# Two heads' matrix products interleaved by kind: maxima, scores and biases of an attention kernel in mixed pairs

## The chip, the core and the metric

The kernel runs on one core of one Trainium2 chip. The metric is the device time of one execution in microseconds (us), from one launch that computes everything. TensorE (PE in the profile) multiplies matrices, with its weight loads shown as PEld; VectorE (DVE), ScalarE (ACT) and GpSimd (POOL) work on elements; SyncE (SP) here only starts the stores of the output.

## What is computed

Attention over 8 batches and 12 heads with 448 tokens of 64 features each, and then a soft mixture of 8 experts with 4 slots each:

```python
scores = scale * np.matmul(q, k.transpose(0, 1, 3, 2))
m = np.max(scores, axis=-1, keepdims=True)
e = np.exp(scores - m)
attn = e / (np.sum(e, axis=-1, keepdims=True) + np.exp(-m) + 1e-09)
attn_out = np.matmul(attn, v)
x = attn_out.transpose(0, 2, 1, 3).reshape(B * S, H * D)
logits = x @ phi                       # 3584 x 32
slot_input = softmax(logits, axis=0).T @ x
slot_out = relu(slot_input @ w1) @ w2  # one pair of matrices for each of 8 experts
out = softmax(logits, axis=1) @ slot_out
```

Inputs and output are float32; the kernel multiplies in bfloat16.

## The kernel before

The 96 heads are handled as 48 pairs (NPAIR). The 64 features of one head of a pair lie in partitions 0 to 63 and those of the other in 64 to 127, so that a product of either head uses half of TensorE's rows, and two such products, one in each half, can run side by side. `hl` is the head in the pair, 0 or 1.

For a pair, four kinds of work go through TensorE:

- `T(n)` transposes q and k of pair n (28 small products, line 205) into one bank of PSUM. ACT (line 208) copies it out for one pair in three, DVE (line 210) for the other two.
- `A(n, i)` makes the row maxima: for one chunk i of 128 queries the products with all 448 keys (line 227, one for each head), each into a bank of its own, and for each a reduction on DVE (line 231) into one column of `mx`. The last chunk, i = 3, has 64 queries for each head and puts both heads into one bank (lines 237 and 240). A pair's four `A` are called runs of maxima here.
- `Bk(n, i)` makes the transposed scores of one chunk i of 128 keys with all queries (line 302, one product for each head), adds the negated maxima to them by a second product with a selecting matrix into the same bank (line 305, called the bias), and takes the exponential on ACT (line 308), one instruction for each head. The chunk i = 3 has 64 keys for each head.
- `AV(n, i, ...)` multiplies the exponentials with v (line 339); `N1` copies the result out (line 351, on ACT for all but the last pairs), `N2` normalises it (lines 360 and 361 on DVE, then lines 367 to 376 on POOL), and `PX` transposes it for the second part of the kernel (line 399, copied out by ACT at line 405).

PSUM's banks come from three pools, each handed out in turn: `psA` with three banks (transposes, maxima products, and the small products of the second part), `psB` with four (scores, `PX`, and the transposed maxima), `psV` with one (`AV`). A product that takes a bank waits until the instruction that empties the bank's former content is through. TensorE takes its products in the order in which they stand in the program, which is written out by hand.

The main loop runs over s = 0 to 48, a step for each pair, with two halves, y = 0 (the early half) and y = 1 (the late half). The scores are those of pair s, the maxima run some pairs ahead: from s = 3 on exactly four pairs, so that at step s the maxima are those of pair s + 4. The list `runs` holds the runs of maxima still to do, and `As(c)` does the next c of them. From s = 3 on a step does this on TensorE:

```python
# y = 0
As(1); Bk(s, 0); Bk(s, 1); As(1)           # maxima 0, scores 0 and 1, maxima 1
AV(s - 1, 2 and 3)                         # with post[2 * s] among it, where there is one
# y = 1
As(1); Bk(s, 2); Bk(s, 3, side=1)          # maxima 2, scores 2, scores 3 with maxima 3 within
T(s + 6); W2 and W3 in every third step; AV(s, 0 and 1); post[2 * s + 1]; PX(s - 2)
```

`W1` (line 247, on POOL) negates the maxima of three pairs, `W2` (lines 267 and 268) transposes them, `W3` (lines 273 to 279) copies them out. `post` holds the parts of the second half of the kernel, spread over the steps of the next batch of six pairs: the logits (line 434, copied by ACT at line 438), their maxima (lines 442, 452, 463, 465), exponentials (lines 474 and 479) and the sums over the tokens (line 489, added by DVE at line 499). After step 47 the experts' matrices, whose last parts are loaded by then, are multiplied and the output is made and stored.

Loads are issued from POOL's queue: q, k and v some steps ahead, and the experts' matrices (line 108) in parts over the whole loop.

Of the kernel before, what the change touches and what calls it, by code (L numbers as in the profile page):

```python
# [8 lines left out]
F32 = mybir.dt.float32  # L9
BF16 = mybir.dt.bfloat16  # L10
AX = mybir.AxisListType
AF = mybir.ActivationFunctionType
# [12 lines left out]
HG = 6  # L25
# [6 lines left out]
def kernel(  # L32
# [10 lines left out]
    nc = tc.nc  # L43
    B, H, S, D = q.shape
# [9 lines left out]
    NPAIR = B * PB  # L54
    NG = NPAIR // NP
    scale = 1.0 / (D ** 0.5)
# [15 lines left out]
    sel = const.tile([128, HG], BF16, name="sel")  # L72
# [6 lines left out]
    NQK, NE, VPN, NATV = 7, 5, HG * 4 * VS, HG * 4 * D  # L79
# [11 lines left out]
    e2_t = [part("e2", i * 2 * S, 2 * S).rearrange("p (h s) -> p h s", h=2) for i in range(NE)]  # L91
# [30 lines left out]
    with ExitStack() as at:  # L122
# [3 lines left out]
        psA = pool("psA", 3, space=PSUM)  # L126
        psB = pool("psB", 4, space=PSUM)
        psV = pool("psV", 1, space=PSUM)
        pb_ = lambda nm: psB.tile([128, 512], F32, tag="b", name=nm)
# [55 lines left out]
        mx, ngm, ec, mT, eT, av, us = {}, {}, {}, {}, {}, {}, {}  # L185
        qkT = {}
        st = {"e2": 0}
# [7 lines left out]
        def T(n):  # L195
            g, pl = divmod(n, NP)
            ps = psA.tile([128, 2, S], BF16, tag="a", name="ps_t")
            for a in range(2):
                src = nat["qk"[a], g]
                for tok in range(7):  # L200
                    for hl in range(2):

                        c = kcol(hl, tok) if a else (2 * tok if tok < 4 else 2 * tok - 7) * 64
                        r = slice(64 * hl, 64 * hl + 64)
                        nc.tensor.transpose(ps[r, a, c:c + 64], src[r, pl, tok * D:(tok + 1) * D], ident[r, r])  # L205
            t = qk_t[n % NQK]
            if n < 6 or pl == 0:
                nc.scalar.copy(t, ps)  # L208
            else:
                nc.vector.tensor_copy(t, ps)  # L210
            qkT[n] = t
# [3 lines left out]
        mg = lambda n: 0 if n == 0 else n // NP + 1  # L215
        mpl = lambda m: ((0, 1), (1, NP))[m] if m < 2 else (0, NP)

        def A(n, i):
            g, pl = mg(n), n % NP
            if pl == mpl(g)[0] and i == 0:  # L220
                mx[g] = psm.tile([128, 21], F32, tag="mx", name="mx")
            t = qkT[n]
            if i < 3:
                pss = [psA.tile([128, 512], F32, tag="a", name="ps_a") for _ in range(2)]
                for hl in range(2):
                    r = slice(64 * hl, 64 * hl + 64)
                    nc.tensor.matmul(pss[hl][:, 0:S], t[r, 0, i * 128:(i + 1) * 128], t[r, 1, :],  # L227
                                     start=True, stop=True)
                for hl in range(2):
                    c = HG * i + 2 * pl + hl  # L230
                    nc.vector.reduce_max(mx[g][:, c:c + 1], pss[hl][:, 0:S], axis=AX.X)  # L231
            else:
                ps = psA.tile([128, 512], F32, tag="a", name="ps_a")

                for hl in range(2):
                    r = slice(64 * hl, 64 * hl + 64)
                    nc.tensor.matmul(ps[64 - 64 * hl:128 - 64 * hl, 0:S], t[r, 0, 384:448], t[r, 1, :],  # L237
                                     start=True, stop=True)
                c = 3 * HG + pl
                nc.vector.reduce_max(mx[g][:, c:c + 1], ps[:, 0:S], axis=AX.X)  # L240
# [39 lines left out]
            ec[g] = e  # L280


        def Bk(n, i, c=0):

            g, pl = divmod(n, NP)
            t = qkT[n]
            rs = [slice(0, 64), slice(64, 128)]
            if i < 3:
                pss = [pb_("ps_b") for _ in range(2)]
                outs = [p[:, 0:S] for p in pss]  # L290
                cols = slice(i * 128, (i + 1) * 128)
                e = e2_t[st["e2"] % NE]
                st["e2"] += 1
                es = [e[:, hl, :] for hl in range(2)]
            else:
                pss = [pb_("ps_b")]
                outs = [pss[0][r, 0:S] for r in rs]
                cols = slice(384, 448)
                es = [e1_t]
            m = cols.stop - cols.start  # L300
            for hl in range(2):
                nc.tensor.matmul(outs[hl], t[rs[hl], 1, cols], t[rs[hl], 0, :], start=True, stop=False)  # L302
            As(c)
            for hl in range(2):
                nc.tensor.matmul(outs[hl], sel[rs[hl], 2 * pl + hl:2 * pl + hl + 1].to_broadcast([64, m]), mT[mg(n)][rs[hl], :],  # L305
                                 start=False, stop=True)
            for p, e in zip(pss, es):
                nc.scalar.activation(e, p[:, 0:S], AF.Exp, scale=scale)  # L308
            for hl in range(2):
                eT[n, i, hl] = es[hl % len(es)]  # L310
# [236 lines left out]
        runs = [(n, i) for n in range(NPAIR) for i in range(4)]  # L547

        def As(c):
            for _ in range(min(c, len(runs))):  # L550
                A(*runs.pop(0))
# [23 lines left out]
        for s in range(NPAIR + 1):  # L575
            for y in range(2):
                hs = 2 * s + y
                early = int(hs < 5)
                As(1)
                if s < NPAIR:  # L580
                    Bk(s, 2 * y)
                    As(early)
                    side = int(y == 1 and len(runs) > 0 and runs[0][1] == 3)
                    Bk(s, 2 * y + 1, side)
                    As(1 - side)
                else:
                    As(1)
                if hs == 1:
                    W1(1)
                if hs < 5:  # L590
                    T(hs + 3)
                if y == 0:
                    if 0 <= s - 1:
                        for i in (2, 3):
                            AV(s - 1, i, range(3))
                else:
                    if 2 <= s < NPAIR - 6:
                        T(s + 6)
                    g = (s + 1) // 3
                    if (s + 1) % 3 == 0 and g < NG:  # L600
                        W2(g + 1)
                        W3(g + 1)
                    if s < NPAIR:
                        for i in (0, 1):
                            AV(s, i, range(3))
                if 2 * s + y in post:
                    post[2 * s + y]()
                if y and 0 <= s - 2 < NPAIR - 2:
                    PX(s - 2)
                if y == 0:  # L610
                    if 0 <= s - 1:
                        for i in range(4):
                            AV(s - 1, i, [3])
                        N1(s - 1)
                        if not on_pool(s - 1):
                            N2(s - 1)
                else:
                    if 0 <= s - 1 and on_pool(s - 1):
                        N2(s - 1)
                As(early)  # L620
                if hs == 1:
                    W2(1)
                    W3(1)
                if hs == 4:
                    W1(2)
            g = (s + 10) // 3
            if s == 1 or (s and s % 3 == 2):
                if g < NG:
                    load(g, "q")
                    load(g, "k")  # L630
            g = (s + 9) // 3
            if s % 3 == 0 and g - 2 < NG:
                V(g - 2)
                if s and g - 1 < NG:
                    load(g - 1, "v")
            if s % 3 == 1:
                if 1 < (s + 2) // 3 < NG:
                    W1((s + 2) // 3 + 1)
                if s == 1:
                    load(2, "v")  # L640
            if s in half_at:
                load_half(half_at[s], 0, w_tile(half_at[s]))
            if s - 1 in half_at:
                load_half(half_at[s - 1], 1)
            for i, z0, z1 in part_at.get(s, ()):
                load_part(i, z0, z1)
# [57 lines left out]
        pss = [pb_("ps_so") for _ in range(2)]  # L704
# [5 lines left out]
        for half in range(2):  # L710
            for bp in range(B // 2):
                o = (half * (B // 2) + bp) * 4
                nc.tensor.matmul(ps_cs[:, o:o + 4], cT[:, bp, half, :, :].rearrange("p b j -> p (b j)"), band,
                                 start=True, stop=True)
# [7 lines left out]
        for half in range(2):  # L722
            hs = slice(half * ND, (half + 1) * ND)
            ps = psA.tile([128, 512], F32, tag="a", name="ps_sel")
# [5 lines left out]
    with ExitStack() as ex:  # L730
        psO = ex.enter_context(tc.tile_pool(name="psO", bufs=4, space=PSUM))
        for bp in range(B // 2):
# [4 lines left out]
            for t0 in range(0, 7, 2):  # L737
                ts = range(t0, min(t0 + 2, 7))
                pss = [psO.tile([128, 2, 512], F32, tag="o", name="ps_o") for _ in ts]
                for hf in range(2):  # L740
                    for t, ps in zip(ts, pss):
                        r = slice(32 * (t % 4), 32 * (t % 4) + NS)
                        nc.tensor.matmul(ps[:, hf, 0:ND], cT[r, bp, t // 4, :, :].rearrange("p b j -> p (b j)"),  # L743
                                         slot_out[r, hf * ND:(hf + 1) * ND], start=True, stop=True)
                for t, ps in zip(ts, pss):
                    dst = o[:, t, :].rearrange("p (h d) -> p h d", h=2)
                    c = cscale[:, t // 4, bp, t % 4:t % 4 + 1]
# [37 lines left out]
```

## Time and profile before

| | |
|---|---|
| time, median of 3 runs | 321.62 us (321.37 to 322.61) |
| time of the profiled execution | 321.49 us |
| its span, first to last instruction | 319.7 us |
| busy: PE, DVE, ACT, POOL | 284.4, 253.0, 250.1, 194.6 us |
| mean granted clock of TensorE | 0.951; 1.00 in every window up to 250 us |
| the maxima's reductions, line 231 | 288 of 615 ns, 160.7 us busy |
| the exponentials, line 308 | 336 of 560 ns, 158.3 us busy |
| maxima products, line 227 | 288, 364 ns each |
| scores and biases of full chunks, lines 302 and 305 | 288 each, 353 and 352 ns |

A row of the profile names the line of the kernel, the engine, the operation, the tile written and the tile read, and the shape; for a product "64*128 64x448" means 64 rows and 128 columns of the array and 448 columns streamed through. Timelines merge instructions of one line that follow each other closely; the count stands behind an x. The end of a product is modelled, and a product's duration is longer than the distance to the next one, since products follow each other while the former is still on its way. In square brackets stands idle time of the whole engine before the row, and what ended it. The window of a stage gives busy times that merge overlapping instructions.

### The profile page before, as it was taken

The numbers are of one execution on the slowest core, as the hardware profiler recorded it, in microseconds if no ns is written. First come the engines' busy times: TensorE is split into PE (matmuls) and PEld (weight loads), VectorE is DVE, ScalarE is ACT, GpSimd is POOL, SyncE is SP. The second block draws the span as 40 slices with busy tenths as digits, with TensorE's granted clock in tenths as the row PEclk, the third lists the DMA queues.
The fourth block names the chain that finished last, engine by engine and source line by source line (L and its number), as shares of the span: only waits on it lengthen the run. The fifth ranks groups of instructions, "written<-read, shape, count | busy, mean of one in ns | idle before, by whom it ended". The sixth has DMA issues, their size and how long they took to land.

```text
span 319.7 us, 12146 instructions
## 1 busy us (share of the span) xinstructions
PE 284.4 (89%) x5072; PEld 165.9 (52%) x5074; DVE 253.0 (79%) x575; ACT 250.1 (78%) x546; POOL 194.6 (61%) x402
## 2 busy tenths in 40 slices
PE   2898999999999999999999999999999997997800
PEld 1444556555566566656656665566555555561100
DVE  5888999998989989997999799989998354337910
ACT  2367699999989998999999999999998983217800
POOL 8651797868768968695978688867775723100000
PEclk9999999999999999999999999999999999897555
DMA  7990799999999999678999999997445899964998
GB/s 87 143 135 4 105 208 203 187 193 162 184 180 162 197 148 180 86 112 146 187 154 187 180 170 162 182 193 130 76 51 100 149 157 193 200 126 178 425 431 344
DMA packets 32838, 54.30 MB, mean 170 GB/s; under 512 B 2576, under 2 KB 27920, under 8 KB 32272
## 3 DMA queue, kind: packets, MB, share of 16 engines
q0 software_dynamic: 31776, 42.52, 81.8%
q1 hardware_dynamic: 1008, 11.01, 8.2%
q8 instruction: 39, 0.64, 0.7%
q14 instruction: 15, 0.12, 0.1%
HBM read 85.03 MB, written 11.01 MB: 300 GB/s over the span
## 4 chain that ended last, share of the span: by engine, by line
PE 53%; DVE 22%; ACT 11%; issue 4%; DMA 3%; POOL 2%; POOLq 0%; ACTq 0%
DVE mx L231 15%; PE ps_b L302 11%; PE ps_av L339 11%; PE ps_a L227 9%; PE ps_b L305 7%; PE ps_t L205 5%; ACT R L308 5%; DMA R<-in_moe_w_dram 3%; PE ps_s L489 3%; PE ps_o L743 3%; ACT R L208 2%; DVE mx L240 2%; DVE R L210 2%; ACT R L405 2%; ACT W L749 2%
## 5 line engine op out<-in xcount | busy, mean ns | idle before, releaser
L308 ACT ACTIVATE R<-ps_b 128x448 bf16<-128x448 f32 x336 | 158.3, 560 | 13.4 <-PE ps_b L305 9.9
L231 DVE TENSOR_REDUCE mx<-ps_a 128x1 f32<-128x448 f32 x288 | 160.7, 615 | 9.5 <-PE ps_a L227 9.0
L302 PE MATMUL ps_b<-R 64*128 64x448 bf16 (+1 forms) x384 | 82.6, 358 | 2.1 <-ACT R L405 1.8
L305 PE MATMUL ps_b<-mT,sel 64*128 64x448 bf16 (+1 forms) x384 | 78.9, 352 | 0.0
L227 PE MATMUL ps_a<-R 64*128 64x448 bf16 x288 | 68.8, 364 | 5.3 <-DVE mx L231 2.9
L367 POOL TENSOR_TENSOR R<-ubuf,rec 128x384 bf16<-128x384 f32 x44 | 36.3, 824 | 47.9 <-DVE rec L361 22.4
L339 PE MATMUL ps_av<-R 128*128 128x65 bf16 (+1 forms) x1536 | 64.8, 196 | 0.1
L339 PEld LDWEIGHTS <-R 128*128 128x128 bf16 (+1 forms) x1536 | 50.2, 100 | 23.9 <-issue 19.7
L205 PEld LDWEIGHTS <-R 64*64 64x64 bf16 x1344 | 31.1, 113 | 16.6 <-issue 6.1
L205 PE MATMUL ps_t<-ident,R 64*64 64x64 bf16 x1344 | 31.5, 197 | 5.3 <-DMA R<-in_q_dram 4.3
L302 PEld LDWEIGHTS <-R 64*128 64x128 bf16 (+1 forms) x384 | 19.4, 97 | 30.5 <-issue 25.6
L305 PEld LDWEIGHTS <-sel 64*128 64x128 bf16 (+1 forms) x384 | 21.3, 97 | 23.2 <-issue 15.9
L405 ACT CAST R<-ps_x 128x512 bf16<-128x512 f32 x47 | 27.9, 593 | 6.3 <-PE ps_x L399 6.2
L240 DVE TENSOR_REDUCE mx<-ps_a 128x1 f32<-128x448 f32 x48 | 29.6, 617 | 0.4 <-PE ps_a L237 0.3
L208 ACT COPY R<-ps_t 128x896 bf16<-128x896 bf16 x20 | 18.4, 918 | 10.8 <-PE ps_t L205 10.8
L351 ACT COPY ubuf<-ps_av 128x455 f32<-128x455 f32 x44 | 25.1, 571 | 1.2 <-PE ps_av L339 1.0
L227 PEld LDWEIGHTS <-R 64*128 64x128 bf16 x288 | 17.8, 94 | 14.5 <-issue 3.6
L376 POOL TENSOR_TENSOR R<-ubuf,rec 128x128 bf16<-128x128 f32 x44 | 17.6, 400 | 3.7
L237 PE MATMUL ps_a<-R 64*64 64x448 bf16 x96 | 18.5, 381 | 0.6 <-DVE mx L231 0.6
L399 PE MATMUL ps_x<-ident,R 128*128 128x128 bf16 x192 | 18.7, 218 | 0.0
L247 POOL TENSOR_SCALAR R<-mx 64x6 bf16<-64x6 f32 (+5 forms) x51 | 13.6, 266 | 8.1 <-DVE mx L231 4.7
L108 POOL DMA_DIRECT2D R<-in_moe_w_dram x15 | 8.4, 566 | 15.7 <-PE ps_s L489 6.7
(126 smaller groups left out, 368.5 us busy)
## 6 DMA issues: line engine op xcount, KB each, us to landing
W<-in_moe_w_dram POOLq DMA_DIRECT2D x22, 768.0 KB, 10.2
out_dram<-W SPq DMA_DIRECT2D x3, 2688.0 KB, 11.2
R<-in_v_dram POOLq DMA_DIRECT2D x32, 192.0 KB, 6.0
R<-in_q_dram POOLq DMA_DIRECT2D x15, 336.0 KB, 6.0
R<-in_k_dram POOLq DMA_DIRECT2D x15, 336.0 KB, 7.3
R<-in_moe_w_dram POOLq DMA_DIRECT2D x3, 768.0 KB, 7.7
out_dram<-W SPq DMA_DIRECT2D x3, 768.0 KB, 4.3
R<-in_moe_w_dram POOLq DMA_DIRECT2D x1, 1344.0 KB, 11.5
```

The costliest lines, as they stand in the source:

```text
L205: nc.tensor.transpose(ps[r, a, c:c + 64], src[r, pl, tok * D:(tok + 1) * D], ident[r, r])
L208: nc.scalar.copy(t, ps)
L227: nc.tensor.matmul(pss[hl][:, 0:S], t[r, 0, i * 128:(i + 1) * 128], t[r, 1, :], start=True, stop=True)
L231: nc.vector.reduce_max(mx[g][:, c:c + 1], pss[hl][:, 0:S], axis=AX.X)
L240: nc.vector.reduce_max(mx[g][:, c:c + 1], ps[:, 0:S], axis=AX.X)
L302: nc.tensor.matmul(outs[hl], t[rs[hl], 1, cols], t[rs[hl], 0, :], start=True, stop=False)
L305: nc.tensor.matmul(outs[hl], sel[rs[hl], 2 * pl + hl:2 * pl + hl + 1].to_broadcast([64, m]), mT[mg(n)][rs[hl], :], start=False, stop=True)
L308: nc.scalar.activation(e, p[:, 0:S], AF.Exp, scale=scale)
L339: nc.tensor.matmul(o, eT[n, i, hl][:, qc], vp[g % 2][:, 2 * pl + hl, i, 0:W65], start=(i == 0 and u == 0 and hl == 0), stop=(i == 3), skip ...
L351: (nc.scalar.copy if on_pool(n) else nc.vector.tensor_copy)(u, src)
L367: eng.tensor_mul(x[:, 0:3, c:c + 128].rearrange("p i (h d) -> p i h d", h=2), u[:, 0:6, 0:D].rearrange("p (i h) d -> p i h d", h=2), rec[: ...
L405: nc.scalar.copy(xT[:, pb, :], pss[0])
```

## The change

`A` gets a form that returns its two products, each with its reduction, as two steps, and `Bk` a form that places them among its own four products. For a full chunk (i < 3) of the scores with a full run of maxima, TensorE's order becomes

- before: maxima 0, maxima 1; score 0, score 1; bias 0, bias 1
- after: maxima 0, score 1; score 0, bias 1; bias 0, maxima 1

where the figure is the head, which is the half of the rows. Each exponential is issued behind its own bias, head 1 first. In the early half the second run of maxima used to stand behind both chunks of scores; now its first product stands ahead of the second chunk's scores and its second behind that chunk's last bias. In the late half the 64-wide chunk with its run of maxima stays as it was. The new order holds for s = 3 to 43, 41 steps with three such chunks each, which is 123 chunks; before s = 3 and after s = 43 the order is the old one. The orders of DVE, POOL and SP stay, and on ACT the two heads of a chunk's exponentials change places.

```diff
--- before.py
+++ after.py
@@ -215,11 +215,22 @@
         mg = lambda n: 0 if n == 0 else n // NP + 1
         mpl = lambda m: ((0, 1), (1, NP))[m] if m < 2 else (0, NP)
 
-        def A(n, i):
+        def A(n, i, steps=False):
             g, pl = mg(n), n % NP
             if pl == mpl(g)[0] and i == 0:
                 mx[g] = psm.tile([128, 21], F32, tag="mx", name="mx")
             t = qkT[n]
+            if steps:
+                m = mx[g]
+
+                def run(hl):
+                    r = slice(64 * hl, 64 * hl + 64)
+                    ps = psA.tile([128, 512], F32, tag="a", name="ps_a")
+                    nc.tensor.matmul(ps[:, 0:S], t[r, 0, i * 128:(i + 1) * 128], t[r, 1, :], start=True, stop=True)
+                    c = HG * i + 2 * pl + hl
+                    nc.vector.reduce_max(m[:, c:c + 1], ps[:, 0:S], axis=AX.X)
+
+                return [lambda: run(0), lambda: run(1)]
             if i < 3:
                 pss = [psA.tile([128, 512], F32, tag="a", name="ps_a") for _ in range(2)]
                 for hl in range(2):
@@ -280,11 +291,36 @@
             ec[g] = e
 
 
-        def Bk(n, i, c=0):
+        def Bk(n, i, c=0, mix=False):
 
             g, pl = divmod(n, NP)
             t = qkT[n]
             rs = [slice(0, 64), slice(64, 128)]
+            if i < 3 and mix and runs and runs[0][1] < 3:
+
+                e = e2_t[st["e2"] % NE]
+                st["e2"] += 1
+                cols = slice(i * 128, (i + 1) * 128)
+                a0, a1 = A(*runs.pop(0), steps=True)
+                pss = {}
+
+                def score(hl):
+                    pss[hl] = pb_("ps_b")
+                    nc.tensor.matmul(pss[hl][:, 0:S], t[rs[hl], 1, cols], t[rs[hl], 0, :], start=True, stop=False)
+
+                def bias(hl):
+                    nc.tensor.matmul(pss[hl][:, 0:S], sel[rs[hl], 2 * pl + hl:2 * pl + hl + 1].to_broadcast([64, 128]),
+                                     mT[mg(n)][rs[hl], :], start=False, stop=True)
+                    nc.scalar.activation(e[:, hl, :], pss[hl][:, 0:S], AF.Exp, scale=scale)
+                    eT[n, i, hl] = e[:, hl, :]
+
+                a0()
+                score(1)
+                score(0)
+                bias(1)
+                bias(0)
+                a1()
+                return
             if i < 3:
                 pss = [pb_("ps_b") for _ in range(2)]
                 outs = [p[:, 0:S] for p in pss]
@@ -576,8 +612,15 @@
             for y in range(2):
                 hs = 2 * s + y
                 early = int(hs < 5)
-                As(1)
-                if s < NPAIR:
+                mix = s >= 3 and len(runs) > 1 and runs[0][1] == 2 * y
+                if mix:
+                    Bk(s, 2 * y, mix=True)
+                    Bk(s, 2 * y + 1, y, mix=True)
+                else:
+                    As(1)
+                if mix:
+                    pass
+                elif s < NPAIR:
                     Bk(s, 2 * y)
                     As(early)
                     side = int(y == 1 and len(runs) > 0 and runs[0][1] == 3)
```

## The prediction

> **What bounds the kernel now.** I read the windows of the page's stage that the change touches first, then its waits, then the timeline of TensorE alone, last the other engines around one stall. The stage is steps s = 3 to 43, 41 steps of about 5.1 us. Its window (columns: length, then busy time of PE, PEld, DVE, ACT, POOL, the granted clock, the DMA share, GB/s):
>
> ```profile
> 39.30:246.70 207.40, 203.29 (x3937) 126.38 (x3934) 190.21 (x431) 194.37 (x441) 159.21 (x320) 1.00 0.97 159
> ```
>
> TensorE looks full, ACT is idle for 13.0 us and DVE for 17.2 us. The waits of the same window make TensorE's own waits look like nothing:
>
> ```profile
> PE ps_b L302 <- ACT R L405: 1.8, 8, 0.3
> PE ps_a L227 <- DVE mx L231: 1.1, 6, 0.2
> ```
>
> They hide it: one product uses half of the array's rows, and while the product of one half waits, the last one of the other half still counts as busy. The timeline of TensorE shows it (start, length, shape, count):
>
> ```profile
> 163.11 0.85 PE L227 MATMUL ps_a<-R 64*128 64x448 bf16 x2
> 163.61 0.53 PE L302 MATMUL ps_b<-R 64*128 64x448 bf16 x2
> ...
> 164.26 0.38 PE L302 MATMUL ps_b<-R 64*64 64x448 bf16 x2
> 164.27 0.38 PE L237 MATMUL ps_a<-R 64*64 64x448 bf16 x2
> ...
> 164.66 0.60 PE L205 MATMUL ps_t<-ident,R 64*64 64x64 bf16 x28
> ...
> 165.89 0.36 PE L227 MATMUL ps_a<-R 64*128 64x448 bf16 x2
> 166.09 0.35 PE L302 MATMUL ps_b<-R 64*128 64x448 bf16 x2
> ...
> 166.47 0.35 PE L302 MATMUL ps_b<-R 64*128 64x448 bf16 x1
> 167.01 0.35 PE L302 MATMUL ps_b<-R 64*128 64x448 bf16 x1 [0.19 <-ACT R L405]
> 167.02 0.53 PE L305 MATMUL ps_b<-mT,sel 64*128 64x448 bf16 x2
> 167.22 0.52 PE L227 MATMUL ps_a<-R 64*128 64x448 bf16 x2
> 167.67 0.79 PE L339 MATMUL ps_av<-R 128*128 128x65 bf16 x20
> 168.39 0.36 PE L227 MATMUL ps_a<-R 64*128 64x448 bf16 x2
> 168.59 0.35 PE L302 MATMUL ps_b<-R 64*128 64x448 bf16 x2
> 168.78 0.35 PE L305 MATMUL ps_b<-mT,sel 64*128 64x448 bf16 x2
> 169.06 0.38 PE L302 MATMUL ps_b<-R 64*64 64x448 bf16 x2
> ```
>
> From 168.39 on is the undisturbed case: a pair takes one pass, 0.20 us for the first, 0.19 for each further, 0.28 for the last before products of another shape. So the early half of a step (six passes) should last 1.24 us and the late half's three 0.67. At 163.11 the second maxima product started 0.50 late, though the row calls it one group of 0.85, and it held back scores that waited for nothing: 1.15 instead of 0.67. At 165.89 the half took 1.78: one score of the second pair waited 0.54 for its bank, and three passes stood behind it. Summed so over all 41 steps, early halves lose 11.0 us and late ones 6.3: 17.3 us in which half of the array stands still.
>
> The rows of the three other engines that the sum below uses, of the unfiltered timeline there and ten us later:
>
> ```profile
> 163.90 1.15 DVE L231 TENSOR_REDUCE mx<-ps_a 128x1 f32<-128x448 f32 x2
> 165.55 0.92 ACT L208 COPY R<-ps_t 128x896 bf16<-128x896 bf16 x1
> 166.33 0.63 ACT L405 CAST R<-ps_x 128x512 bf16<-128x512 f32 x1
> 173.41 0.96 POOL L247 TENSOR_SCALAR R<-mx 128x36 bf16<-128x36 f32 x3
> ```
>
> **What the change moves.** No instruction is added or dropped, DVE's and POOL's orders stay, and ACT only swaps the heads of an exponential pair. On TensorE 123 chunks (41 steps by 3) go from pairs of like products to a0+s1, s0+b1, b0+a1 (a maxima, s score, b bias, the figure is the head). Cost of the pairs themselves: nothing, six products are three passes either way, and the pairs occur already where a stall had skewed two halves. The row at 163.61 shows a score started 6 ns after the late maxima product, at 167.02 a bias product runs beside a score, at 167.22 a maxima beside a bias, and the next pass still comes 0.19 to 0.20 later. Two things differ: a waiting second maxima product no longer has its chunk's scores and biases behind it, and ACT's first exponential needs the second pass, not the third, so it may start 0.19 earlier. Against that, a maxima product now stands ahead of the second chunk's scores.
>
> **The sum,** followed from 163 to 182, the free part of a six-step cycle of 30.7 us. Releases read off the rows: a product is usable 0.39 after its start, a reduction frees its bank 0.66 after its start, reductions follow each other at 0.53.
> - Late half, 163.11. The second maxima product still starts at 163.61, since DVE sets that, but the rest is through: the 64-column step starts at 163.89, not 164.26. The transposes need the bank of the reduction of 163.90: 164.57 instead of 164.66, so TensorE keeps only 0.09. ACT keeps more: its bias is ready at 163.31 + 0.39 = 163.70, ACT is free of the copy before at 163.96, against 164.26: 0.30.
> - So L208 starts at 165.24 and L405 at 166.02, and the waiting score at 166.70 rather than 167.01. Behind it now stand two passes instead of three: last pass 166.89, next kind 167.17 instead of 167.67. Gain 0.50.
> - Next step: nothing waits in its late half; transposes 0.48 earlier; the last maxima product of the early half at 170.72 waits for DVE as before. Gain still 0.48.
> - Its late half at 172.93: DVE lets the second maxima product go at 172.98 instead of 173.46; the 64-column step comes 0.28 after that, at 173.26 instead of 174.11. Gain 0.85.
> - There POOL limits: L247 ends at 174.37, and the product that needs its last part was at 175.23 and comes to 174.38 to 174.41. Its slack is used up; 0.82 stays.
> - Early half at 175.94, now 175.12: the last maxima product waits for the first reduction, 175.12 + 0.40 + 0.66 = 176.18, next kind 176.46 instead of 177.39. Gain 0.93. DVE, idle for 1.40 us at 180.2 until TensorE's L489 is through, takes this over.
>
> From 181 to 193 the reductions are back to back (one idle of 0.28 us), and TensorE's waits there are DVE's in both orders: I take nothing. Where a stall goes is hence clear: to the last maxima product of the early half, which waits for the reduction of the first.
>
> Moving a maxima product ahead of a score costs nothing as long as its bank, freed by the copy of the last transposes, is free 0.58 after the half's start: slack 0.17 us where ACT copies (L208 from 165.24 to 166.21 with its release, due 166.38), about 0.24 where DVE does.
>
> Taking 0.9 us per six steps, 41 steps give 6.2 us. The profiled execution was 321.49 us, its span 319.7, so 1.8 lie around it; the median is 321.62, the same within 0.1%. Forecast 321.5 - 6.2 = 315.3. The start and the end of the kernel keep their length and shift.
>
> **Rivals.**
> - *Evacuation sets the pace.* DVE is at 92% and ACT at 94% of the stage, and the gain of 0.30 or 0.84 goes into waits for reductions. Against it: both engines have idle rows that TensorE ended (1.40 us above). If only the two 0.09 us ends survive, 0.2 per six steps, the gain is 1.4 and the time 320.1. [...] The trace half agrees: from 181 to 193 it is so, from 163 to 181 not.
> - *Slower: a maxima product blocks the second chunk's scores.* Its bank waits for the copy of the transposes. In the order of before, L208 ended at 166.47, exactly when the new order wants it. If L208 starts later than 0.39 us before the half, scores and thus ACT wait. One ACT instruction too late, 0.42 us, in every third step: 14 times 0.42 is 5.9 us, 327.4. For it: DVE and ACT have little room. Against it: the sum above starts L208 0.56 us before the half.
> - *Slower by much: pairs of unlike products don't run side by side.* Each of 123 x 3 passes would take 0.19 more: 70 us, 391. The rows at 163.61, 167.02 and 167.22 speak against it; so it is left with little. That the change does nothing is excluded, since TensorE's order does change in 123 places.
> - *All goes well.* The gain is bounded by ACT's idle 13.0 us: 308.5.
>
> **How the numbers follow.** Forecast 0.64; evacuation 0.20, half of it below the 0.5% (1.6 us) that a measurement can tell from no change; blocked scores 0.08; serial pairs 0.04; all gained 0.04. Faster by over 0.5%: 0.64 + 0.04 + 0.11 = 0.79; within: 0.09; slower: 0.12. The range takes the forecast with its size uncertain from under half (a gain of 2.5) to 10.5, and the evacuation case's 320.1, and leaves out the two slower cases and the best one: 311.0 to 321.0.
>
> **What would show it.** Right: L227's second product no longer holds L302 back; late halves last 0.67 or end 0.28 after the last maxima product; the early halves' first exponential starts about 0.59 after the half's first product instead of 0.77; ACT's busy share of the stage rises from 94% to 96%; waits of "PE ps_a L227" for DVE move to the end of the early half. Wrong: a first maxima product of a chunk waiting for L208 or L210 with scores behind it; a pass longer than 0.20 us; DVE's idle time in the stage not falling from 17.2 us by about 6.

## The result, and the profile after

The changed kernel takes 317.16 us (median of 19 runs, 315.17 to 320.55), the kernel before 321.9 us in the same session (19 runs, 320.79 to 323.26): the ratio is 0.9842 [0.982, 0.9863], a gain of about 5 us or 1.6%. The ratio leaves out the two slowest of the 19 runs, the profiled one among them. The forecast was 315.3 us in a range of 311.0 to 321.0. The profiled execution of the changed kernel took 320.22 us, span 318.4; it lost nearly 5 us at the very end, to a load that came late. Its stage of 41 steps is within 1.0 us of the others', so the stage is read here and the end apart.

The window of the stage, after (length, then busy time of PE, PEld, DVE, ACT, POOL, the granted clock, the DMA share, GB/s):

```profile
40.20:242.00 201.80, 200.96 (x3951) 125.18 (x3948) 188.98 (x433) 192.35 (x443) 159.00 (x321) 1.00 0.99 164
```

The stage lost about 6 us. ACT's idle time went from 13.0 to 9.45 us (201.80 - 192.35), DVE's from 17.2 to 12.8. Two waits that DVE and ACT had for TensorE in the stage of before, from the view of waits of that window,

```profile
DVE mx L231 <- PE ps_a L227: 5.9, 22, 0.6
ACT R L308 <- PE ps_b L305: 3.6, 12, 0.3
```

are nearly gone in the same view after:

```profile
DVE mx L231 <- PE ps_a L229: 1.8, 7, 0.3
ACT R L314 <- PE ps_a L229: 0.2, 1, 0.2
```

The timeline of TensorE after, at about the place of the prediction's rows (L229 maxima, L309 scores, L312 biases, L338, L341 and L248 the 64-column scores, biases and maxima, L205 the next pair's transposes, L375 `AV`):

```profile
160.51 0.35 PE L229 MATMUL ps_a<-R 64*128 64x448 bf16 x1
160.51 0.53 PE L309 MATMUL ps_b<-R 64*128 64x448 bf16 x2
160.71 0.52 PE L312 MATMUL ps_b<-mT,sel 64*128 64x448 bf16 x2
161.04 0.35 PE L229 MATMUL ps_a<-R 64*128 64x448 bf16 x1
161.31 0.38 PE L338 MATMUL ps_b<-R 64*64 64x448 bf16 x2
...
161.53 0.35 PE L341 MATMUL ps_b<-mT,sel 64*64 64x448 bf16 x2
162.00 0.63 PE L205 MATMUL ps_t<-ident,R 64*64 64x64 bf16 x28
...
163.25 0.36 PE L229 MATMUL ps_a<-R 64*128 64x448 bf16 x1
163.25 0.55 PE L309 MATMUL ps_b<-R 64*128 64x448 bf16 x2
163.45 0.54 PE L312 MATMUL ps_b<-mT,sel 64*128 64x448 bf16 x2
163.64 0.54 PE L229 MATMUL ps_a<-R 64*128 64x448 bf16 x2
...
164.32 0.35 PE L229 MATMUL ps_a<-R 64*128 64x448 bf16 x1
164.60 0.79 PE L375 MATMUL ps_av<-R 128*128 128x65 bf16 x20
```

The late half at 160.51 is the stalled kind: its second maxima product comes 0.53 later, where it was 0.50 in the kernel before, but scores and biases have gone through meanwhile, and the 64-column step follows 0.27 after it, 0.80 from the half's start. The early half at 163.25 lasts 1.35: its last maxima product, at 1.07, closes it alone.

Adding up every half beyond its undisturbed length (1.24 and 0.67 us), and the time from one kind of product to the next for all of TensorE, gives the whole account of the stage, first maxima product of s = 3 to last full one of s = 43:

| us | before | after |
|---|---|---|
| stalls in 41 early halves | 10.98 | 6.92 |
| stalls in 41 late halves | 6.32 | 1.65 |
| last 64-column bias to the transposes, summed | 7.31 | 9.63 |
| stage | 205.56 | 199.36 |
| a cycle of six steps, in the steady part | 30.67 | 29.83 |

The halves gave 8.7 us; 2.3 came back as a wait of the transposes for their bank, which a reduction empties (the row at 162.00 comes 0.47 after the last bias, where 0.19 is the undisturbed distance); every other sum, such as that of the `AV` products, is the same within 0.4 us. What is left, 6.4, is nearly the 6.2 us of the stage. In the five other profiled executions with the new order (experiments 2 and 7 to 10) the stage took 199.7 to 200.4, a gain of 5.1 to 5.9. Experiment 9 shows where such a difference can lie: in one step TensorE stands idle for 0.88 us, from 210.47, for no cause that the profile shows.

Then the end. The chain of waits of before and of after, and the timeline of TensorE after, all around the last load of the experts' matrices and the 41 products that need it:

```profile
275.17 11.12 DMA R<-in_moe_w_dram
...
286.34 1.96 PE ps_so L687 x41
```
```profile
269.12 14.46 DMA R<-in_moe_w_dram
283.62 3.44 PE ps_so L730 x36
```
```profile
278.79 1.30 PE L730 MATMUL ps_so<-R,W 128*32 128x384 bf16 x24
283.62 3.42 PE L730 MATMUL ps_so<-R,W 128*32 128x384 bf16 x41 [3.53 <-DMA R<-in_moe_w_dram]
```

The load was issued 6.05 us earlier than before, and the last of the products that need nothing of it began 6.06 earlier (278.79 against 284.85). But the load took 14.46 us instead of 11.12; TensorE stood idle for 3.53 us, and then the 41 products took 3.42 instead of 1.95 us, with the granted clock at 0.50 up to 286.6, where it was 1.00 before the change. So 6.06 - 3.4 - 1.5, about 1.2 us, was left of the gain in that execution: 321.49 - 320.22.

That 6.06 is so near to the 6.2 of the stage is chance, as the span taken apart shows (with experiments 7 and 9, the changed kernel again):

| us | before | after | 7 | 9 |
|---|---|---|---|---|
| start, up to the first maxima product of s = 3 | 39.35 | 40.58 | 40.50 | 39.48 |
| stage | 205.56 | 199.36 | 200.06 | 200.36 |
| from there to the experts' first product (L673, L716) | 30.56 | 29.47 | 30.55 | 30.25 |
| experts' products, up to L725 or L768 | 12.76 | 17.57 | 12.88 | 13.26 |
| the rest | 31.47 | 31.47 | 31.46 | 31.47 |

The start took 39.2 to 39.5 us in seven of the thirteen profiles and 40.5 to 40.8 in six, with executions of both orders in each group. In the six, the 28 transposes at 22.2 us still take 0.96 us as those before them do; in the seven, those at 21.4 to 21.7 take 0.63. The third row has two lengths too, of which the three profiles with the order of before have only the longer; the last section shows the clock there.

### The profile page after: what moved, and what is told of

Its sections match the earlier page's. It is cut to its first block, busy times and chain, and to the rows that moved or that the text cites. A ratio compares the mean times of both kernels' runs of the same rounds, so it can differ in the third digit from the quotient of the medians.

```text
span 318.4 us, 12144 instructions
## 1 busy us (share of the span) xinstructions
PE 282.9 (89%) x5072; PEld 165.1 (52%) x5074; DVE 251.1 (79%) x575; ACT 247.3 (78%) x546; POOL 194.0 (61%) x402
## 4 chain that ended last, share of the span: by engine, by line
PE 67%; DVE 14%; ACT 5%; DMA 5%; issue 3%; POOL 2%; POOLq 0%; ACTq 0%
PE ps_av L375 15%; PE ps_a L229 10%; PE ps_t L205 7%; PE ps_b L309 6%; PE ps_b L312 6%; DVE mx L231 6%; PE ps_b L338 5%; DMA R<-in_moe_w_dram 5%; PE ps_b L341 3%; DVE mx L242 3%; PE ps_x L435 3%; PE ps_s L525 3%; PE ps_o L786 2%; ACT W L792 2%; PE ps_a L238 2%
## 5 line engine op out<-in xcount | busy, mean ns | idle before, releaser
L314 ACT ACTIVATE R<-ps_b 128x448 bf16<-128x448 f32 x246 | 118.5, 576 | 0.2 <-PE ps_a L229 0.2
L229 PE MATMUL ps_a<-R 64*128 64x448 bf16 x246 | 79.9, 351 | 0.0
L309 PE MATMUL ps_b<-R 64*128 64x448 bf16 x246 | 67.8, 352 | 0.3
L312 PE MATMUL ps_b<-mT,sel 64*128 64x448 bf16 x246 | 65.5, 350 | 0.0
L375 PE MATMUL ps_av<-R 128*128 128x65 bf16 (+1 forms) x1536 | 65.1, 196 | 0.1
L375 PEld LDWEIGHTS <-R 128*128 128x128 bf16 (+1 forms) x1536 | 50.4, 101 | 27.5 <-issue 23.2
L344 ACT ACTIVATE R<-ps_b 128x448 bf16<-128x448 f32 x90 | 47.6, 573 | 7.1 <-PE ps_b L341 7.0
L205 PEld LDWEIGHTS <-R 64*64 64x64 bf16 x1344 | 31.2, 113 | 18.8 <-issue 7.5
L205 PE MATMUL ps_t<-ident,R 64*64 64x64 bf16 x1344 | 32.0, 198 | 5.6 <-DMA R<-in_q_dram 4.1
L441 ACT CAST R<-ps_x 128x512 bf16<-128x512 f32 x47 | 28.2, 600 | 7.9 <-PE ps_x L435 7.9
L251 DVE TENSOR_REDUCE mx<-ps_a 128x1 f32<-128x448 f32 x48 | 29.5, 615 | 0.6 <-PE ps_a L248 0.3
L338 PE MATMUL ps_b<-R 64*64 64x448 bf16 (+1 forms) x138 | 28.9, 380 | 0.1
L229 PEld LDWEIGHTS <-R 64*128 64x128 bf16 x246 | 23.1, 94 | 9.8
L208 ACT COPY R<-ps_t 128x896 bf16<-128x896 bf16 x20 | 18.8, 941 | 11.3 <-PE ps_t L205 11.0
L341 PE MATMUL ps_b<-mT,sel 64*64 64x448 bf16 (+1 forms) x138 | 27.0, 362 | 0.0
L312 PEld LDWEIGHTS <-sel 64*128 64x128 bf16 x246 | 20.0, 94 | 12.4 <-issue 2.2
L338 PEld LDWEIGHTS <-R 64*64 64x64 bf16 (+1 forms) x138 | 7.3, 101 | 23.2 <-issue 22.1
```

What stands on the lines that cost most here:

```text
L229: nc.tensor.matmul(ps[:, 0:S], t[r, 0, i * 128:(i + 1) * 128], t[r, 1, :], start=True, stop=True)
L309: nc.tensor.matmul(pss[hl][:, 0:S], t[rs[hl], 1, cols], t[rs[hl], 0, :], start=True, stop=False)
L312: nc.tensor.matmul(pss[hl][:, 0:S], sel[rs[hl], 2 * pl + hl:2 * pl + hl + 1].to_broadcast([64, 128]), mT[mg(n)][rs[hl], :], start=False, s ...
L314: nc.scalar.activation(e[:, hl, :], pss[hl][:, 0:S], AF.Exp, scale=scale)
L375: nc.tensor.matmul(o, eT[n, i, hl][:, qc], vp[g % 2][:, 2 * pl + hl, i, 0:W65], start=(i == 0 and u == 0 and hl == 0), stop=(i == 3), skip ...
```

## The experiments

Several theories stood. T: the order works through its waits, as in the prediction's walk. L: part of the gain, or the missing part of it, is the last load. S: each stall is worth its length. V: the stage itself varies from run to run. M: only the mixing of kinds counts. P: it only counts that the maxima stand behind. The variants called light leave out the load of seven of the eight parts of the last expert's second matrix, so that the end doesn't blur them, and don't compute the whole output; e1 and e2 are the two kernels in that form.

**1 and 2. Both kernels without the last load.**

```diff
-        load_part(15, 1, 5)
-        load_part(15, 5, 8)
```

> The kernel before, without its last two loads of the last expert's second matrix (seven of that matrix's eight row groups are left out, 1344 KB). Theory T (the attention stage gave 6.06 us, and what the end gives back is a race between TensorE and the last load): before, TensorE waited 0.19 us for that load, so 321.4. Rival L (the loads bound the end in both kernels): over 2 us below the kernel before.

> The changed kernel, with the same two loads left out. T: the whole gain of the attention stage arrives, 6.1 us below the light kernel before, 315.3, in every run within about 0.5 us. Rival V (the attention stage itself varies from run to run): the runs spread from 315 to 320 as those of the changed kernel do.

Before without it: 321.8 us (10 runs, 319.98 to 323.36), ratio 0.9975 [0.995, 1.0]. After without it: 316.3 (4 runs, 315.43 to 317.04), ratio 0.9809 [0.9776, 0.9841]. The load costs the kernel before next to nothing, so the gain isn't the load's. The changed kernel's median is 0.9 lower without it, but the intervals of the two ratios overlap, and the forecast is 1.0 lower still. That the runs lie closer together without the load isn't shown: the four here lie within 1.6 us, the four of experiment 7, with the load, within 0.6. V holds in part: the stage took 199.4 to 200.4 us in the six profiles of the changed order.

**3 and 4. The new order in one half of each step only**, both light.

```diff
-                mix = s >= 3 and len(runs) > 1 and runs[0][1] == 2 * y
+                mix = y == 1 and s >= 3 and len(runs) > 1 and runs[0][1] == 2 * y
```

and `y == 0` in the other.

> The light kernel with the new order in the late halves alone (y = 1). Walking the six-step cycle as in the prediction: ACT's 0.30 us earlier at 163 arrives at the waiting score of the next early half (0.31), and the late half at 172.93 adds 0.37: 0.68 us per six steps, 4.6 us in all, 316.8. Rival S (each stall is worth its length, so that the early halves, which lose 11.0 us, count more than the late ones with 6.3): under 3 us of gain, over 318.4.

> The light kernel with the new order in the early halves alone (y = 0). By the same walk: 0.19 us behind the score that waits for L405, 0.09 at the last maxima product of the early half at 175.94: 0.3 us per six steps, 2.0 us in all, 319.4. Rival S: over 3 us of gain, under 318.4.

The late half alone: 318.86 us (7 runs), 0.9889 [0.9854, 0.9924]; the early half alone: 320.61 (10 runs), 0.9955 [0.9933, 0.9978]. By the first maxima product of each step in the profiles:

| us | before, light | late only | early only | both |
|---|---|---|---|---|
| first 8 steps | 39.3 | 39.1 | 38.2 | 37.9 |
| a steady cycle of six steps | 30.67 | 29.97 | 30.47 | 29.8 |
| stage | 205.32 | 202.20 | 203.30 | 200.19 |
| stalls, early and late halves | 10.96, 6.30 | 9.48, 1.43 | 8.47, 6.92 | 6.86, 1.63 |

The steady cycle gains 0.70 from the late half (the walk says 0.68) and 0.20 from the early (0.3). Each half's stalls shrink where its order is changed, those of the late half to a quarter. Both times missed all the same: 318.86 for 316.8 and 320.61 for 319.4. What I missed with experiment 3 is the multiplication: its cycle doesn't hold for all 41 steps, as the first eight steps gain only 0.2 from the late half, and 1.1 from the early one; and step 38 alone was 0.5 us longer than in the light kernel before. By its time experiment 3 is on S's side (over 318.4), but S said that the early halves count more, and they gave less. The two stages add up, in one profiled execution each: 3.1 + 2.0 us, and both together gain 5.1.

**5. The second maxima product in the middle** of the three pairs, the kinds still mixed (light).

```diff
                 a0()
                 score(1)
                 score(0)
+                a1()
-                bias(1)
                 bias(0)
-                a1()
+                bias(1)
```

> The light kernel with another order of unlike pairs: a0+s1, s0+a1, b0+b1, so that the second maxima product again stands ahead of its chunk's biases. Theory T (it is the place of the second maxima product that counts, and ACT's start with the second pass): half of the gain is lost, about 3 us remain, 318.3. Rival M (it is the mixing of kinds in a pass that counts): all of it stays, 315.3.

321.45 us (10 runs, 318.98 to 323.41), 0.9976 [0.9947, 1.0006]: the gain is gone. M is out. T said 318.3, and missed by the other half of the gain. The timeline of TensorE in this kernel, an early half:

```profile
165.89 0.35 PE L229 MATMUL ps_a<-R 64*128 64x448 bf16 x1
165.90 0.79 PE L309 MATMUL ps_b<-R 64*128 64x448 bf16 x2
166.39 0.35 PE L229 MATMUL ps_a<-R 64*128 64x448 bf16 x1
166.53 0.39 PE L312 MATMUL ps_b<-mT,sel 64*128 64x448 bf16 x2
166.85 0.79 PE L375 MATMUL ps_av<-R 128*128 128x65 bf16 x20
```

The chunk's second maxima product waits till 166.39, 1.08 after the half's start at 165.31, and the two biases follow only at 166.53: the half lasts 1.54, against 1.35 in the new order. Summed, early halves stall for 14.6 us, more than before the change (11.0); late ones are down to 1.75. The steady cycle is 30.61.

**6. Like pairs, maxima last** (light): no mixing at all, but the waiting products stand at the end.

```diff
+                score(0)
+                score(1)
+                bias(0)
+                bias(1)
                 a0()
-                score(1)
-                score(0)
-                bias(1)
-                bias(0)
                 a1()
```

> The light kernel with pairs of like kinds and the maxima behind: s0+s1, b0+b1, a0+a1. No maxima product holds back a score or a bias of its chunk, and ACT starts with the second pass. Theory T: slower than before, since the first maxima product, and with it DVE, comes 0.39 us later in every half: the last maxima product of the early half waits until 1.45 us instead of 1.07, and the transposes for the reduction of the late half's first product: 0.3 to 0.6 us a step over 41 steps, 332 to 345. Rival P (all that matters is that maxima products stand behind scores and biases): as fast as the changed kernel, 315.3.

340.13 us (4 runs), 1.0573 [1.0535, 1.0611], within T's range; P is out. The timeline of TensorE there:

```profile
165.31 0.35 PE L341 MATMUL ps_b<-mT,sel 64*64 64x448 bf16 x2
165.88 0.63 PE L205 MATMUL ps_t<-ident,R 64*64 64x64 bf16 x28 [0.22 <-DVE mx L231]
...
168.66 0.35 PE L229 MATMUL ps_a<-R 64*128 64x448 bf16 x1 [0.22 <-DVE mx L231]
```

DVE gets its first banks two passes later (the first maxima product at 167.52 in the half that starts at 167.13, 0.39 us), so both the last maxima product of the half and the transposes wait for it. Of the four orders measured, only that of the change lets one maxima product go at once and the other last; like pairs with the maxima in the middle were not tried.

**7 to 11. The end.** The changed kernel twice more (7 and 9), and both kernels with the last part of the final products' order changed: first all that doesn't need the last load, for both halves of the output, then what does (8 and 10 on the changed kernel, 11 on the one before).

```diff
-            slots(1, range(FK), [half])
+            slots(1, range(5), [half])
+        for half in range(2):
+            slots(1, range(5, FK), [half])
```

> The changed kernel itself, to compare the next one with on one chip. T: 315.3 to 320, depending on how long the last load takes.

> The changed kernel with the products of the second expert group (L730) in another order: row groups 0 to 4 for both halves of the columns first, then 5 to 7 for both, so that 40 products instead of 20 stand ahead of the wait for the last load. T (the last load and TensorE race at the end): where the load is late, the 20 products (about 0.95 us) move into the wait: 0.5 to 1 us below the changed kernel in the median. Rival: no difference, as the load ends in time in most runs, or slower by up to 0.3 us, since the copy of the first column half then has 12 instead of 32 products to hide behind.

> The changed kernel once more, beside the next two on one chip. T: 315.3 to 320, median 317.

> The changed kernel with the reordered second expert group once more. T: 0.5 to 1.3 us below the changed kernel of the same call. If the difference of the first comparison (1.35 us) came from where the half clock fell, none is left.

> The kernel before with the same reordered second expert group. Its TensorE waited only 0.19 us for the last load in the profiled execution, so the two theories part: if the load is late only after the change, no difference (321.6 to 322.1); if the load is late in many executions of both, 0.5 to 1 us faster.

| | us, median and range | ratio to before, run beside it |
|---|---|---|
| 7, after | 317.25 (316.95 to 317.55) | 0.9855 [0.9828, 0.9883] |
| 8, after, split | 315.9 (315.11 to 316.95) | 0.9817 [0.9786, 0.9848] |
| 9, after | 316.67 (314.99 to 318.65) | 0.9826 [0.9789, 0.9863] |
| 10, after, split | 316.19 (315.82 to 316.63) | 0.9813 [0.9786, 0.984] |
| 11, before, split | 321.72 (320.5 to 323.16) | 0.9988 [0.9964, 1.0013] |

The last products in 9 and in 8, from the timelines of TensorE:

```profile
281.47 1.95 PE L730 MATMUL ps_so<-R,W 128*32 128x384 bf16 x41 [0.70 <-DMA R<-in_moe_w_dram]
```
```profile
280.75 1.14 PE L730 MATMUL ps_so<-R,W 128*32 128x384 bf16 x21 [0.78 <-DMA R<-in_moe_w_dram]
```

TensorE waits for the load in both, but with the split only 21 products come after it instead of 41, 0.8 us less. That agrees with the medians (0.5 to 1.35 lower), but the intervals overlap, so a gain by the split isn't shown. The profiled execution of 8 was 2.14 us shorter than that of 7, but not by the split: its start was 1.23 shorter and the stretch after the stage 1.05, and from the experts' first product on it took 0.5 longer (44.82 us against 44.34). The split version has the lowest medians here of what computes everything, about 6 us below before; for the kernel before the split does nothing that can be told.

## Why the prediction was right, point by point

- *What bounds the kernel: stalls that the view of waits hides.* Right. 17.3 us of stalls became 8.6. In the changed kernel the view of waits lists no wait of PE for DVE at `ps_a` at all, though the early halves' last maxima product waits in each step; the prediction expected to see these there, which contradicts its own reading of that view.
- *Cost of the pairs themselves: nothing.* Right. In the early half at 163.25 the passes start at 0, 0.20, 0.39: no pass became longer.
- *The late half.* Right to 0.02 us: second maxima product at +0.53 (0.50 before), the 64-column step 0.27 behind it (0.28 said). The transposes wait for a reduction, as said: 2.3 us in all.
- *The early half.* Next kind at 1.34 said; of the six early halves from 152 to 178 three took 1.35 and three 1.43 to 1.46, with the last maxima product at 1.07 and at 1.15 to 1.19.
- *POOL limits in every third step.* It does, in the late half at 169.92: L258 ends at 171.77 and the product that needs its last part starts at 171.85, where before 0.86 us lay between.
- *Gain per cycle.* Walked to 0.93, taken as 0.9; measured 0.84. As the walk has it, the gain lies in three of the six steps; the other three keep their length within 0.1 us. The stage gains 5.1 to 6.2, where 6.2 was said. That one execution gave just 6.2 is luck: 0.84 over 41 steps would be 5.7, and the first eight steps gained 1.8 there instead of the cycle's 1.1.
- *A maxima product ahead of a score costs nothing.* Right: no first maxima product of a chunk waits for L208 or L210 from 156 to 172, and the second chunk's scores come 0.58 after the half's start, as in an undisturbed half. The first exponential starts 0.65 after the late half shown (at 161.16) and 0.69 after the early one (at 163.94), for which 0.59 was said; before the second, ACT is at its copy L441 until then.
- *ACT's share and DVE's idle time.* 95.3% for 96% and 12.8 for about 11. Here the sizes were a little off: DVE's 433 instructions also took 1.8 us less.
- *The start and the end keep their length and shift.* This step failed. The last load is issued with the shift but isn't through with it. TensorE waits 0.31, 0.70 and 3.53 us for it in the three profiles of the changed kernel, 0.19 before. Nor does the start keep its length, nor the stretch after the stage: each has two lengths, over 1 us apart at the start and about 1 us after the stage, and executions of the changed kernel differ in both. Experiment 7's execution has about the median time and is 1.95 us over the forecast: 1.15 of the start, 0.7 of the stage and 0.1 of the experts' products. Experiment 9's is 1.3 over: 1.0 of the stage and 0.5 of the experts' products, with 0.2 won back in the rest. So the 1.9 us by which the median was off have no single cause, and how they divide over all runs is not known; the range had room for them.

Of the rivals, *evacuation sets the pace* (320.1) is out as a whole: it left 1.4 us of the gain, and the stage gained 5.1 to 6.2. But the 2.3 us returned at the transposes are of that kind: a bank that a reduction has yet to empty. *Blocked scores* and *serial pairs* don't show.

## What to carry to other kernels

When two products share the array by rows, a wait of one need not show as idle time in the lists: here 17.3 us of stalls stood beside 1.8 and 1.1 us in the view of waits. Look at the distance between starts and compare it with an undisturbed group. Where products are taken in program order, let the product whose bank comes free last stand last, and the one whose reader is the busiest first; pairing unlike kinds lets one chunk do both (light: 316.3 us in this order, 321.8 in that of before, 321.45 with the second maxima product in the middle, 340.13 with both last). A part alone need not scale from its steady cycle: the late half's 0.70 us per six steps would be 4.8 over 41, and its stage gave 3.1. A transfer that just arrived in time can be the next bound once the work ahead of it gets shorter: TensorE waited 0.19 us for the last load before the change, and 0.31 to 3.53 after it. And take a profiled execution apart before its time is compared with another's: here the start and the stretch after the stage moved by about 1 us each between executions of one kernel.

## What the runs showed of the hardware

The wait for the late load was followed by slow products. After 3.53 us of idle TensorE the same 41 products took 3.42 us, and in experiment 9, after 0.70 us, 1.95. A window of the changed kernel's profile, with the granted clock in the third column from the end:

```profile
284.00:285.00 1.00, 1.00 (x20) 0.58 (x16) 0.22 (x1) 0.00 (x0) 0.00 (x0) 0.50 0.00 0
```

The clock stood at 0.50 for 3.4 us, from 283.2 to 286.6; the products began at 283.62. Half clock also followed a shorter wait. In experiment 9 TensorE waits 1.65 us for a copy (L441) behind the last `AV` products, and soon after its clock is at 0.50 for 3.4 us:

```profile
263.80 0.24 PE L466 MATMUL ps_lT<-R,phi_sb 128*32 128x128 bf16 x4 [1.65 <-ACT R L441]
264.50:267.90 3.40, 3.40 (x18) 1.34 (x17) 1.53 (x5) 0.70 (x3) 0.56 (x1) 0.50 1.01 203
```

The same wait, 1.54 to 1.67 us, is in all thirteen profiles; nine have a stretch of half clock at it, and four (the changed kernel's first, 5, 6 and 8) have none. From the stage's end to the experts' first product the nine took 30.3 to 31.0 us, the four 29.1 to 29.5. What decides between the two was not tried.

The load itself was long for its last packets. From 280.2 on its packets of 4608 B (361 ns each) came one by one, the last from 281.22 to 281.58; the DMA share of 0.07 to 0.08 is that of about one of the sixteen engines. Then a 16 KB packet of the instruction queue took 962 ns from 281.57, and the load's last small packet came behind it and ended at 282.54. The landing followed at 283.58, 1.04 us later, where 0.3 us lay between in the kernel before and in experiments 7 and 9. The order of these packets is in the trace; that the instruction packet is the cause was not tried, and what the last 1.04 us were is open.
